# Issuing the second weight part earlier, and one unit's turn, scores and outputs later, in a fused attention and FFN kernel

## The chip, the cores and the metric

One core of one Trainium2 chip. The metric is the device time of one execution in microseconds (us); lower is better. The kernel before takes 318.6 us (median of the first four runs, 318.35 to 320.92).

## The reference, cut to what matters

```python
# q, k, v: (8 batches, 8 heads, 576 tokens, 64) float32; w_in (512, 2048), w_out (2048, 512) float32
scores = (q @ k.T) / 8
ret = scores * Dmat          # causal decay: gamma_h ** (i - j) for i >= j, else 0
x = (ret @ v) -> (4608, 512) # heads side by side
h = x @ w_in
g = where(h > 0, h, exp(min(h, 0)) - 1)
out = g @ w_out              # (4608, 512) float32
```

## The kernel before

The kernel cuts the 4608 tokens into 36 *units* of 128. A unit's raw q, k and v (256 KB each) are loaded by SP's DMA queue. ACT, DVE or POOL cast q and k to bf16, and POOL scales v. PE *turns* q and k (eight transposes, copied out of PSUM by DVE and ACT), makes the *scores*, and the *outputs* (three sets of matmuls named inter, state and intra), which DVE multiplies into `x`. FFN1 follows for a group of units: per tile four matmuls with one 128-column slice of w_in each, then `e` on ACT, `m` on POOL and `g` on DVE. FFN2 follows that. Weights are cast while they are loaded, on POOL's DMA queue, w_in in four parts of 512 columns. The first group is units 0 to 2, and its FFN1 has 16 tiles of 384 tokens, called tile 0 to tile 15 here. Tiles 0 to 3 need w_in part 1, tiles 4 to 7 part 2, and so on. (In the code the parts are numbered from 0.)

The order in which the program lists an engine's instructions is what the change moves. The parts that matter:

```python
def load(u, after=None):                    # SP queue: q, k, v of unit u
    qk = raw.tile(...); vv = raw.tile(...)
    if after is not None:
        after.memset(qk[0:1, 0, 0, 0:1], 0.0)   # holds the load back until this engine is here
    ...
    nc.sync.dma_start(dst, src[...])        # 256 B runs
def load_w_in(n):                           # POOL queue, float32 -> bf16
    nc.gpsimd.dma_start(w_in_sb[:, :, s], w_in_v[:, :, s])
...
for u in range(4):
    load(u)
...                                         # constants
def finish(n=0):                            # g of the tiles that are n slots old, on DVE; frees the tile's bank
    while late and late[0][0] <= slot[0] - n:
        ...
        nc.vector.scalar_tensor_tensor(gt_, ph, 0.0, m, ALU.max, ALU.min)
...
def dummy(n):                               # matmuls that only keep PE busy
    dum = ps_m.tile([P, 512], FP32, name="dum", tag="pm")
...
for u in range(3):
    scores(u); inter(u); state(u); masks(u)
    if u < 2:
        cast(u + 1, A, G)
        if u == 0:
            load_w_in(0)
        scale_v(u + 1)
        dummy(3)
        turn(u + 1, h)
    else:
        for n in range(1, 4):
            load_w_in(n)
        load_w_out(0, 0, 8); load_w_out(0, 8, 16); load_w_out(1, 0, 16)
        dummy(3)
    intra(u); put_x(u); state_out(u); dummy(2)
cast(3, A, V)                               # unit 3: q on ACT, k on DVE, ahead of every e and g below
for n in range(16):                         # tiles 0 to 15
    f1(0, n, m if n % 4 == 3 else None)     # three "h" banks, and "m" for every fourth tile
    if n == 3: turn(3)
    if n == 5: scale_v(3)
    if n == 7: scores(3); masks(3, 0)
    if n == 8: masks(3, 1)
    if n == 9: load(4, nc.vector) ...       # units 4 to 11
    if n == 11: product(3)
for n in range(4):
    f1(1, n, m if n == 3 else None)         # FFN1 of unit 3
finish()
for u, bank in enumerate((h, h, h, m)): ffn2_half(u, 0, bank)
prep(4, A, G); ffn2_half(0, 1, h); turn(4); ...
```

`cast(3, A, V)` stands ahead of the FFN1 tiles in the program. ACT and DVE therefore do nothing for these tiles before unit 3's q and k have landed. A tile's PSUM bank comes free only when DVE has made its `g`, and there are four banks, so tile 4 cannot start before DVE is past its cast.

Of the kernel before, what the change touches and what calls it, by code (L numbers as in the profile page):

```python
# [9 lines left out]
FP32 = mybir.dt.float32  # L10
# [7 lines left out]
def kernel(  # L18
# [14 lines left out]
    P = 128  # L33
# [3 lines left out]
    NU = B * S // P  # L37
# [8 lines left out]
    PE_TURNED = 12  # L46
# [23 lines left out]
    ps_m = ctx.enter_context(tc.tile_pool(name="ps_m", bufs=1, space=PSUM))  # L70
    ps_s = ctx.enter_context(tc.tile_pool(name="ps_s", bufs=1, space=PSUM))
# [22 lines left out]
    def load_w_in(n):  # L94
        s = slice(n * 512, (n + 1) * 512)
        nc.gpsimd.dma_start(w_in_sb[:, :, s], w_in_v[:, :, s])
# [65 lines left out]
    def cast(u, *engs):  # L162

        rqk, _ = raws[u]
        n = nat.tile([P, 2, H * D], BF16, name="qkn", tag="qkn")
        src = rqk.rearrange("p c h d -> p c (h d)")
        if len(engs) == 1:
            engs[0](n, src)  # L168
        else:
            for c in range(2):  # L170
                engs[c](n[:, c], src[:, c])
        kns[u] = n

    def scale_v(u):
        _, rv = raws[u]
        n = nat.tile([P, H, D], BF16, name="vn", tag="vn")
        nc.gpsimd.tensor_tensor(  # L177
            n, rv, gk[:, u % R].unsqueeze(2).to_broadcast([P, H, D]), ALU.mult
        )
        vns[u] = n  # L180

    def turn(u, bank=None):

        t = tpool.tile([P, 2, HP, P], BF16, name="qkT", tag="qkT")
        n = kns[u]
        if u < PE_TURNED:
            if bank:
                pool, tag = bank
                ps = [pool.tile([P, HP, P], BF16, name="tr", tag=tag) for c in range(2)]
            else:  # L190
                both = ps_s.tile([P, 2, 2, HP, P], BF16, name="tr", tag="sc")
                ps = [both[:, c, 0] for c in range(2)]
            for c in range(2):
                for hp in range(HP):
                    nc.tensor.transpose(ps[c][:, hp], n[:, c, hp * P : (hp + 1) * P], ident)  # L195
            nc.vector.tensor_copy(t[:, 0], ps[0])  # L196
            nc.scalar.copy(t[:, 1], ps[1])  # L197
        else:
            nc.sync.dma_start_transpose(
                t.rearrange("p c h t -> p (c h) t"), n.rearrange("p c f -> p (c f)")  # L200
            )
        qkTs[u] = t

    def scores(u):
        t = qkTs[u]
        sc = ps_s.tile([P, 2, HP, P], FP32, name="sc", tag="sc")
        for hp in range(HP):
            for j in range(2):
                for i in range(2):
                    r = slice(i * D, (i + 1) * D)  # L210
                    nc.tensor.matmul(  # L211
                        sc[j * 64 : (j + 1) * 64, i, hp], t[r, 1, hp, j * 64 : (j + 1) * 64], t[r, 0, hp],
                        start=(hp == 0), stop=(hp == HP - 1), skip_group_check=True,
                    )
        scs[u] = sc

    def masks(u, i=None):

        if u not in pts:
            pts[u] = ppool.tile([P, 2, HP, P], BF16, name="pt", tag="pt")  # L220
        m = mask[:, 1 if u % R == 4 else 0]
        s = slice(0, 2) if i is None else slice(i, i + 1)
        nc.vector.tensor_tensor(  # L223
            pts[u][:, s].rearrange("p i h t -> p (i h) t"), scs[u][:, s].rearrange("p i h t -> p (i h) t"),
            m.unsqueeze(1).to_broadcast([P, (s.stop - s.start) * HP, P]), ALU.mult,
        )

    def inter(u):

        o = ps_o.tile([P, HP, P], FP32, name="o", tag="o")  # L230
        os_[u] = o
        r = u % R
        if r == 0:
            return
        n = 64 if r == 4 else P
        for hp in range(HP):
            for i in range(2):
                rows = slice(i * D, (i + 1) * D)
                nc.tensor.matmul(  # L239
                    o[rows, hp, :n], sbs[u][rows, hp], qkTs[u][rows, 0, hp, :n],  # L240
                    start=(hp == 0), stop=False, skip_group_check=True,
                )

    def state(u):

        r = u % R
        if r == 8:
            return
        if r in (0, 4):
            sts[0] = ps_st.tile([P, HP, D], FP32, name="st", tag="st")  # L250
        st = sts[0]
        rows = slice(64, P) if r == 4 else slice(0, P)
        for hp in range(HP):
            for i in range(2):
                h = 2 * hp + i
                nc.tensor.matmul(  # L256
                    st[i * D : (i + 1) * D, hp], kns[u][rows, 1, h * D : (h + 1) * D], vns[u][rows, h],
                    start=(hp == 0 and r in (0, 4)), stop=(r in (3, 7)), skip_group_check=True,
                )

    def state_out(u):
        if u % R == 8:
            return
        s = ppool.tile([P, HP, D], BF16, name="sb", tag="sb")
        nc.scalar.copy(s, sts[0])  # L265
        sbs[u + 1] = s

    def intra(u):
        o = os_[u]
        for hp in range(HP):  # L270
            for i in range(2):
                h = 2 * hp + i
                nc.tensor.matmul(  # L273
                    o[i * D : (i + 1) * D, hp], vns[u][:, h], pts[u][:, i, hp],
                    start=(u % R == 0 and hp == 0), stop=(hp == HP - 1), skip_group_check=True,
                )
# [3 lines left out]
    def put_x(u):  # L280
        g, i = group_of[u]
        if i == 0:
            xts[g] = xpool.tile([P, KJ, 512], BF16, name="xt", tag="xt")
        r = u % R
        s0 = P * r if r < 5 else 64 + P * (r - 5)
        nc.vector.tensor_tensor(  # L286
            xts[g][:, :, i * P : (i + 1) * P], os_[u], gx[:, :, s0 : s0 + P], ALU.mult
        )

    def stretch(u, ahead=True):  # L290

        ahead = ahead and u + 1 < NU
        if ahead:
            scores(u + 1)
        inter(u)
        state(u)
        intra(u)
        if ahead:
            masks(u + 1)
        put_x(u)  # L300
        state_out(u)


# [74 lines left out]
    def ffn2_half(u, c, bank):  # L378
        ffn2_cols(u, c * 256, c * 256 + 256, bank, A if u % 2 else V, nc.scalar)


    V, A, G = nc.vector.tensor_copy, nc.scalar.copy, nc.gpsimd.tensor_copy

    def dummy(n):
        dum = ps_m.tile([P, 512], FP32, name="dum", tag="pm")
        for _ in range(n):
            nc.tensor.matmul(dum, warm[:, :P], warm, start=True, stop=True)  # L387

    def prep(u, *engs):
        if u < NU:  # L390
            cast(u, *engs)
            scale_v(u)
# [8 lines left out]
    def product(u):  # L401
        inter(u)
        state(u)
        intra(u)
        put_x(u)
        state_out(u)

    h, m = (ps_h, "ph"), (ps_m, "pm")


    dummy(18)
    cast(0, A, V)
    make_gx()
    scale_v(0)
    turn(0, h)
    dummy(2)
    for u in range(3):
        scores(u)
        inter(u)
        state(u)  # L420
        masks(u)
        if u < 2:
            cast(u + 1, A, G)
            if u == 0:
                load_w_in(0)
            scale_v(u + 1)
            dummy(3)
            turn(u + 1, h)
        else:
            for n in range(1, 4):  # L430
                load_w_in(n)
            load_w_out(0, 0, 8)
            load_w_out(0, 8, 16)
            load_w_out(1, 0, 16)
            dummy(3)
        intra(u)
        put_x(u)
        state_out(u)
        dummy(2)
# [3 lines left out]
    def f1(g, n, bank=None):  # L443
        k = 512 // (P * len(GROUPS[g]))
        ffn1(g, k * n, bank)

    for n in range(16):
        f1(0, n, m if n % 4 == 3 else None)
        if n == 3:
            turn(3)  # L450
        if n == 5:
            scale_v(3)
        if n == 7:
            scores(3)
            masks(3, 0)
        if n == 8:
            masks(3, 1)
        if n == 9:
            load(4, nc.vector)
            for u in range(5, 12):  # L460
                load(u)
        if n == 11:
            product(3)
    for n in range(4):
        f1(1, n, m if n == 3 else None)
    finish()
# [8 lines left out]
    prep(5, A, G)  # L475
    ffn2_half(2, 1, h)
    product(4)
    turn(5)
    ffn2_half(3, 1, m)
    scores(5)  # L480
    masks(5)
    prep(6, A, G)
    f1(2, 0)
    f1(2, 1)
    turn(6)
    f1(2, 2)


    slots, start, now = [(f1, 2, 3, 1.0)], {}, 1.0
# [38 lines left out]
    for f, g, s, d in slots:  # L528
        while events and events[0][0] <= now + d / 2:
            _, kind, u = events.pop(0)  # L530
# [11 lines left out]
    u = NU - 1  # L542
# [31 lines left out]
```

## Time and profile before

| | before |
|---|---|
| median of runs | 318.6 us |
| span of the profiled execution | 318.0 us |
| PE busy | 307.1 us, 97% |
| chain of waits: PE's share | 82% |
| PE idle before tile 4 (timeline) | 2.26 us |
| unit 3's k cast on DVE | 19.4 us |
| FFN1 of unit 3 done, FFN2 begins | 37.9 us |

These lines are from the page of the kernel before: the busy time of each engine with its share of the span, the busy tenths of PE in 40 slices of the span, the granted PE clock in tenths of full speed in the same slices, and the engines' shares of the chain that ended last.

```profile
PE 307.1 (97%) x2974; PEld 174.2 (55%) x3011; DVE 187.4 (59%) x297; ACT 136.9 (43%) x254; POOL 144.9 (46%) x223
...
PE   8969999999999999999999999999999999999995
...
PEclk9998999999999999999999999999999999999999
...
PE 82%; DMA 6%; issue 3%; POOL 3%; SPq 2%; DVE 2%; ACT 0%; POOLq 0%; DVEq 0%
```

PE is the bound, and it is full except in the first slices. A slice is 8 us. In the third (16 to 24 us) PE was busy six tenths, and in the fourth (24 to 32 us) the clock digit is 8: PE idled first and then ran below full speed.

The next lines are PE's timeline of the kernel before: start, duration, line and operation, and in brackets the idle time just before and what ended it. L329 is an FFN1 matmul, L195 a turn and L370 an FFN2 half.

```profile
17.56 2.76 PE L329 MATMUL ph<-xt,w_in_sb 128*128 128x384 bf16 x16 [0.24 <-DVE xt L286]
20.15 0.61 PE L195 MATMUL tr<-ident,qkn 128*128 128x128 bf16 x8
23.02 4.46 PE L329 MATMUL ph<-xt,w_in_sb 128*128 128x384 bf16 x16 [2.26 <-DMA w_in_sb<-in_moe_w_in_dram]
...
37.92 8.90 PE L370 MATMUL pmh<-w_out_sb,g 128*128 128x256 bf16 x80
```

Tiles 0 to 3 (16 matmuls) end near 20.3 us, the turn of unit 3 fills 0.6 us, and PE then waits for w_in part 2. Tiles 4 to 7 take 4.46 us from 23.02, where tiles 0 to 3 took 2.76 us: most of them ran at half speed.

DVE's timeline of the kernel before shows the cast of unit 3's k with its DMA, and the first two `g`:

```profile
19.40 0.72 DVE L171 CAST qkn<-rqk 128x512 bf16<-128x512 f32 x1 [1.90 <-DMA rqk<-in_k_dram]
20.51 1.04 DVE L313 SCALAR_TENSOR_TENSOR g<-ph,m 128x384 bf16<-128x384 f32 x2 [0.39 <-POOL m L336]
```

Last, the DMA queues of the kernel before in two stretches of one microsecond, 14 to 15 us and 16 to 17 us: packets, MB, and their time as a share of 16 engines. q0 carries the weights, q1 the raw tiles.

```profile
q0 software_dynamic: 156, 0.16, 93.6%
q1 hardware_dynamic: 153, 0.04, 29.6%
```

```profile
q1 hardware_dynamic: 1088, 0.27, 124.2%
```

Beside weight packets of 1 KB, q1 moved 153 packets of 256 B. Alone it moved 1088. Unit 3's 3 x 1,024 packets went through mostly while q0 was empty, from about 15.5 to 17.9 us.

### The profile page before, as it was taken

What the parts mean: (1) busy time and instruction counts of PE and PEld (TensorE: products, weight loads), DVE (VectorE), ACT (ScalarE), POOL (GpSimd) and SP (SyncE); (2) the same over time, 40 slices, a digit from 0 to 9 for tenths busy, and PEclk for the clock granted to TensorE, in tenths of its full rate; (3) what the DMA queues carried; (4) which work ended last, traced back from release to release, by engine and by line L of the source; (5) the groups of instructions that cost most, each with busy time, mean ns of one, the idle gap of its engine ahead of it and who ended that gap; (6) DMA issues with size and microseconds to landing.
All of it is one profiled execution on the core that took longest, in us unless ns stands there. A gap on an engine that the chain in (4) does not pass through costs nothing.

```text
span 318.0 us, 7546 instructions
## 1 busy us (share of the span) xinstructions
PE 307.1 (97%) x2974; PEld 174.2 (55%) x3011; DVE 187.4 (59%) x297; ACT 136.9 (43%) x254; POOL 144.9 (46%) x223
## 2 busy tenths in 40 slices
PE   8969999999999999999999999999999999999995
PEld 3535888877766555555444444444444444444444
DVE  2755724667768777776677666666666655444300
ACT  6435514654643444444444444344444444344411
POOL 2875633555645655544554444444444433333300
PEclk9998999999999999999999999999999999999999
DMA  9999999999999998999999859778224200000111
GB/s 170 215 220 201 197 206 253 205 202 202 207 233 188 233 224 179 168 235 195 170 212 170 171 123 207 166 166 170 69 66 69 66 35 33 35 33 33 66 69 66
DMA packets 150195, 48.72 MB, mean 153 GB/s; under 512 B 138640, under 2 KB 146192, under 8 KB 150160
## 3 DMA queue, kind: packets, MB, share of 16 engines
q1 hardware_dynamic: 141888, 41.76, 67.5%
q0 software_dynamic: 6256, 4.19, 8.8%
q10 hardware_dynamic: 2016, 2.29, 2.2%
q8 instruction: 23, 0.38, 0.5%
q14 instruction: 12, 0.10, 0.1%
HBM read 36.70 MB, written 9.44 MB: 145 GB/s over the span
## 4 chain that ended last, share of the span: by engine, by line
PE 82%; DMA 6%; issue 3%; POOL 3%; SPq 2%; DVE 2%; ACT 0%; POOLq 0%; DVEq 0%
PE ph L329 35%; PE pm L354 31%; PE pmh L370 6%; PE sc L211 3%; DMA w_in_sb<-in_moe_w_in_dram 3%; PE o L273 2%; SPq L86 2%; PE st L256 2%; PE o L239 2%; DMA rv<-in_v_dram 2%; DMA qkT<-qkn 1%; POOL m L336 1%; POOL vn L177 1%; DVE pt L223 1%; PE tr L195 1%
## 5 line engine op out<-in xcount | busy, mean ns | idle before, releaser
L336 POOL TENSOR_SCALAR m<-e 128x512 bf16<-128x512 f32 (+1 forms) x156 | 93.7, 601 | 142.0 <-ACT e L334 137.1
L329 PE MATMUL ph<-xt,w_in_sb 128*128 128x512 bf16 (+3 forms) x816 | 146.5, 315 | 3.9 <-DMA w_in_sb<-in_moe_w_in_dram 2.3
L313 DVE SCALAR_TENSOR_TENSOR g<-ph,m 128x512 bf16<-128x512 f32 (+1 forms) x156 | 100.2, 647 | 81.3 <-POOL m L336 80.3
L334 ACT ACTIVATE e<-ph 128x512 f32<-128x512 f32 (+1 forms) x156 | 87.9, 564 | 124.6 <-PE ph L329 119.8
L354 PE MATMUL pm<-w_out_sb,g 128*128 128x512 bf16 x478 | 122.8, 379 | 1.5 <-issue 0.8
L329 PEld LDWEIGHTS <-w_in_sb 128*128 128x128 bf16 x832 | 71.8, 98 | 59.5 <-issue 4.0
L354 PEld LDWEIGHTS <-g 128*128 128x128 bf16 x496 | 47.8, 98 | 53.2 <-issue 0.2
L223 DVE TENSOR_TENSOR pt<-sc,mask 128x1024 bf16<-128x1024 f32 (+1 forms) x37 | 44.2, 1194 | 14.6 <-PE sc L211 14.4
L177 POOL TENSOR_TENSOR vn<-rv,gk 128x512 bf16<-128x512 f32 x36 | 37.9, 1052 | 1.8 <-DMA rv<-in_v_dram 1.3
L286 DVE TENSOR_TENSOR xt<-o,gx 128x512 bf16<-128x512 f32 x36 | 24.5, 682 | 3.1 <-PE o L273 2.9
L361 ACT COPY ot<-pm 128x512 f32<-128x512 f32 x31 | 18.1, 585 | 14.5 <-PE pm L354 13.8
L370 PE MATMUL pmh<-w_out_sb,g 128*128 128x256 bf16 (+1 forms) x176 | 18.3, 263 | 0.0
L265 ACT CAST sb<-st 128x256 bf16<-128x256 f32 x32 | 11.9, 373 | 13.1 <-PE st L256 11.3
L211 PEld LDWEIGHTS <-qkT 64*64 64x64 bf16 x576 | 9.2, 106 | 14.0 <-issue 7.8
L370 PEld LDWEIGHTS <-g 128*128 128x128 bf16 x176 | 15.7, 98 | 1.9
L168 DVE CAST qkn<-rqk 128x1024 bf16<-128x1024 f32 x24 | 16.6, 691 | 0.0
L211 PE MATMUL sc<-qkT 64*64 64x128 bf16 x576 | 15.1, 222 | 0.7 <-ACT qkT L197 0.5
L273 PE MATMUL o<-pt,vn 128*64 128x128 bf16 x288 | 14.4, 222 | 0.0
L375 DVE COPY oth<-pmh 128x256 f32<-128x256 f32 (+1 forms) x6 | 2.4, 400 | 18.0 <-PE pmh L370 18.0
L387 PE MATMUL dum<-warm 128*128 128x512 bf16 x32 | 11.2, 473 | 1.4 <-DVE warm L108 1.3
L239 PE MATMUL o<-qkT,sb 64*64 64x128 bf16 (+1 forms) x256 | 12.3, 214 | 0.0
L197 ACT COPY qkT<-tr 128x512 bf16<-128x512 bf16 x12 | 7.0, 585 | 9.6 <-DVE qkT L196 5.9
(40 smaller groups left out, 90.1 us busy)
## 6 DMA issues: line engine op xcount, KB each, us to landing
rqk<-in_q_dram SPq DMA_DIRECT2D x32, 256.0 KB, 4.7
rqk<-in_k_dram SPq DMA_DIRECT2D x32, 256.0 KB, 5.0
rv<-in_v_dram SPq DMA_DIRECT2D x32, 256.0 KB, 5.1
out_dram<-ot SPq DMA_DIRECT2D x27, 256.0 KB, 2.3
w_in_sb<-in_moe_w_in_dram POOLq DMA_DIRECT2D x4, 512.0 KB, 9.2
out_dram<-oth ACTq DMA_DIRECT2D x9, 128.0 KB, 4.0
w_out_sb<-in_moe_w_out_dram POOLq DMA_DIRECT2D x2, 512.0 KB, 14.6
w_out_sb<-in_moe_w_out_dram POOLq DMA_DIRECT2D x1, 1024.0 KB, 22.9
```

What stands on the lines that cost most here:

```text
L177: nc.gpsimd.tensor_tensor(n, rv, gk[:, u % R].unsqueeze(2).to_broadcast([P, H, D]), ALU.mult)
L211: nc.tensor.matmul(sc[j * 64 : (j + 1) * 64, i, hp], t[r, 1, hp, j * 64 : (j + 1) * 64], t[r, 0, hp], start=(hp == 0), stop=(hp == HP - 1) ...
L223: nc.vector.tensor_tensor(pts[u][:, s].rearrange("p i h t -> p (i h) t"), scs[u][:, s].rearrange("p i h t -> p (i h) t"), m.unsqueeze(1).t ...
L239: nc.tensor.matmul(o[rows, hp, :n], sbs[u][rows, hp], qkTs[u][rows, 0, hp, :n], start=(hp == 0), stop=False, skip_group_check=True,)
L273: nc.tensor.matmul(o[i * D : (i + 1) * D, hp], vns[u][:, h], pts[u][:, i, hp], start=(u % R == 0 and hp == 0), stop=(hp == HP - 1), skip_g ...
L286: nc.vector.tensor_tensor(xts[g][:, :, i * P : (i + 1) * P], os_[u], gx[:, :, s0 : s0 + P], ALU.mult)
L313: nc.vector.scalar_tensor_tensor(gt_, ph, 0.0, m, ALU.max, ALU.min)
L329: nc.tensor.matmul(ph[:, i * n : (i + 1) * n], w_in_sb[:, j, f : f + P], xts[g][:, j, :n], start=(j == 0), stop=(j == KJ - 1), skip_group_ ...
L334: nc.scalar.activation(e[:, w], ph[:, w], AF.Exp)
L336: nc.gpsimd.tensor_scalar(m[:, w], e[:, w], -1.0, 1.0, ALU.add, ALU.mult)
L354: nc.tensor.matmul(pm, gts[g, ft][:, it * P : (it + 1) * P], w_out_sb[:, ft], start=(ft == 0), stop=(ft == NFT - 1))
L370: nc.tensor.matmul(pm, gts[g, ft][:, it * P : (it + 1) * P], w_out_sb[:, ft, c0:c1], start=(ft == 0), stop=(ft == NFT - 1),)
```

## The change

The intent is to end PE's wait before tile 4. The second w_in part is issued right behind the first. Unit 3's turn, scores and outputs move some tiles later, because its raw tiles will be later. Two pairs of dummies go into the waits that are left. In the later units the order of scores, masks and `x` changes too.

```diff
+def dummy(n, bank=(ps_m, "pm")):            # was: always the "pm" bank
 for u in range(3):
     scores(u); inter(u)
-    state(u)
     masks(u)
     if u < 2:
         cast(u + 1, A, G)
         if u == 0:
             load_w_in(0)
+            load_w_in(1)
         ...
     else:
-        for n in range(1, 4):
+        for n in range(2, 4):
             load_w_in(n)
         ...
+    state(u)
     intra(u) ...
 for n in range(16):
     f1(0, n, ...)
-    if n == 3: turn(3)
+    if n == 3: dummy(2, (ps_s, "sc"))
     if n == 5: scale_v(3)
-    if n == 7: scores(3); masks(3, 0)
-    if n == 8: masks(3, 1)
+    if n == 7: turn(3); dummy(2, (ps_s, "sc"))
     ...
-    if n == 11: product(3)
+    if n == 11: scores(3); masks(3, 0)
+    if n == 12: masks(3, 1)
+product(3)
 ... cut: in stretch(), for units turned on PE, scores(u + 1) and masks(u + 1) go behind intra(u) and put_x(u);
 ... FFN2 halves, turns and scores of units 5 and 6 change places
```

More of the change, by code (lines that the diff above doesn't have):

```diff
@@ L288, in put_x, with stretch @@
         )
-    def stretch(u, ahead=True):
-        ahead = ahead and u + 1 < NU
-        if ahead:
+    def stretch(u):
+        turned = u + 1 < PE_TURNED
+        if u + 1 < NU and not turned:
             scores(u + 1)
@@ L297, in stretch @@
         intra(u)
-        if ahead:
+        if turned:
+            scores(u + 1)
+            put_x(u)
             masks(u + 1)
-        put_x(u)
+        else:
+            if u + 1 < NU:
+                masks(u + 1)
+            put_x(u)
         state_out(u)
@@ L382 @@
     V, A, G = nc.vector.tensor_copy, nc.scalar.copy, nc.gpsimd.tensor_copy
-    def dummy(n):
-        dum = ps_m.tile([P, 512], FP32, name="dum", tag="pm")
+    def dummy(n, bank=(ps_m, "pm")):
+        dum = bank[0].tile([P, 512], FP32, name="dum", tag=bank[1])
         for _ in range(n):
@@ L449 @@
         if n == 3:
-            turn(3)
+            dummy(2, (ps_s, "sc"))
         if n == 5:
@@ L453 @@
         if n == 7:
-            scores(3)
-            masks(3, 0)
-        if n == 8:
-            masks(3, 1)
+            turn(3)
+            dummy(2, (ps_s, "sc"))
         if n == 9:
@@ L462 @@
         if n == 11:
-            product(3)
+            scores(3)
+            masks(3, 0)
+        if n == 12:
+            masks(3, 1)
+    product(3)
     for n in range(4):
@@ L477 @@
     product(4)
+    ffn2_half(3, 1, m)
+    f1(2, 0)
     turn(5)
-    ffn2_half(3, 1, m)
+    prep(6, A, G)
+    f1(2, 1)
     scores(5)
     masks(5)
-    prep(6, A, G)
-    f1(2, 0)
-    f1(2, 1)
+    f1(2, 2)
     turn(6)
-    f1(2, 2)
     slots, start, now = [(f1, 2, 3, 1.0)], {}, 1.0
```

## The prediction

> What bounds the kernel. PE is busy 97% of 318 us (engine table) and is 82% of the chain of waits, so only what idles or slows PE counts. The one large hole is at the start: the timeline has PE idle 2.26 us before 23.02, released by the second w_in part (issued 14.62, landed 22.98). The next eleven or so FFN1 matmuls take 0.32 us instead of 0.16 (granted clock 0.83 in the window 20 to 30), about 1.8 us more. The hole costs about 4 us. The Trainium skill, "TensorE: Matmul & The Clock Gate", part 1, says that idling halves the clock until some 3.4 us of work; here the half-speed stretch is 3.6 us.
>
> Intent: w_in part 2, issued near 10.7, lands near 20, before tile 4 wants it (20.7). Four dummies cost 0.2 us each, partly inside waits.
>
> What I think it does. The DMA rings are full (share over 1.0 from 2 us on). By quarter microseconds the DMA view shows, from 14.0 to 15.25, 40 packets of the weight queue to 40 of the raw-load queue: round robin by packet, as the skill's "DMA: Bandwidth & Descriptors", queues section, has it. But weight packets are 1 KB and raw-load packets 256 B, so raw loads get 160 packets/us beside weights, against 1,080 alone. Before, unit 3's raw tiles (3 x 1,024 packets) pass through a gap in the weight queue from 15.5 to 17.9: q landed 18.2, k 19.4. Now the second part fills that gap: 1,024 weight packets from 12.2 last until about 18.7, and the third part (still issued 14.6, 3.3 us to its first packet) is waiting by 18. So unit 3's q should land near 21, its k near 26 to 28 (240 packets/us beside w_out's 512 B packets from 25), its v near 31.
>
> The change did not move unit 3's casts: ACT's comes before the first exponential, DVE's (the k half) before the first g. DVE would sit before that cast until about 27, so no h bank is freed, and tile 4 (which needs tile 0's bank) starts near 28 instead of 23.0, on a cold clock: about +5 us. Then the dummies behind the turn share the turn's bank and wait for its two copies (about 1 us), and the product right before f1(1,0) exposes its 0.69 us multiply. f1(1,0) started near 34.3 before; I expect 39 to 42.5.
>
> Gains: putting x before the masks in turned units frees x 1.2 us earlier (the mask multiply's time); the PE waits it can remove between 50 and 100 us total about 0.5 us. From 100 us on nothing changes; PE is bound and absorbs nothing.
>
> Sum: about +8 us if the gap closes fully, +3 to +5 if a gap in the weight queue remains, -2 if unit 3's loads are hardly delayed. I weight these 0.5, 0.25, 0.25. Predicted 324.5 us, 317 to 328. Faster by over 2%: 0.03; within 2%: 0.50; slower by over 2%: 0.47.
>
> Right would show as: waits list a long "DVE qkn <- DMA rqk k" (5 us or more), PE's tile 4 released by DVE g, not by w_in; weight queue without gap from 12 to 34; low clock from 28 to 32; PE waiting before the dummies after the turn and before f1(1,0). Wrong: unit 3's k cast before 22 us, PE idle under 1 us at tile 4.
>
> What would make it wrong: the third part's descriptors starting later than 18.7, so raw loads slip through; arbitration that favours raw loads when two weight parts queue.

## The result, and the profile after

The changed kernel takes 330.56 us (median of four runs, 329.87 to 330.92) against 318.6 us. The ratio is 1.0358, with a 95% interval of 1.0314 to 1.0401: slower. A ratio here is the mean time of one kernel's runs over that of the other's runs of the same rounds, so it is not quite the ratio of the medians. Executions over 1.5% slower than the fastest of the same kernel are left out of the means.

These are the page's lines of the changed kernel, the same four as before:

```profile
PE 308.7 (94%) x2978; PEld 174.9 (53%) x3015; DVE 186.8 (57%) x297; ACT 136.7 (42%) x254; POOL 144.7 (44%) x223
...
PE   8944889999999999999999999999999999999996
...
PEclk9995999999999999999999999999999999999999
...
PE 86%; DMA 5%; SPq 3%; DVE 3%; issue 1%; ACT 1%; DVEq 0%
```

PE's work is the same (308.7 against 307.1 us busy), but the third and fourth PE digits fell to 4, and the fourth clock digit is 5.

PE's timeline of the changed kernel follows; its line numbers are five higher (L334 is FFN1, L392 a dummy, L375 an FFN2 half).

```profile
17.52 2.76 PE L334 MATMUL ph<-xt,w_in_sb 128*128 128x384 bf16 x16 [0.24 <-DVE xt L286]
20.33 0.38 PE L392 MATMUL dum<-warm 128*128 128x512 bf16 x1
29.26 4.71 PE L334 MATMUL ph<-xt,w_in_sb 128*128 128x384 bf16 x16 [8.55 <-DVE g L318]
...
35.55 0.59 PE L392 MATMUL dum<-warm 128*128 128x512 bf16 x2 [1.13 <-ACT qkT L197]
...
43.82 3.73 PE L334 MATMUL ph<-xt,w_in_sb 128*128 128x128 bf16 x64 [0.79 <-DVE xt L286]
47.39 8.90 PE L375 MATMUL pmh<-w_out_sb,g 128*128 128x256 bf16 x80
```

Tile 4 now starts at 29.26 us instead of 23.02, and DVE's `g` is what it waited for, not w_in. Tiles 4 to 7 again run partly at half speed: the trace's clock record has the granted clock at 0.5 from 23.0 to 33.3 us. Behind the turn, PE waits 1.13 us before the dummies. The first matmul of unit 3's FFN1 waits 0.79 us for `x`. The FFN2 halves begin at 47.39 us instead of 37.92. Of the 10.2 us by which the two profiled spans differ, 9.47 us are there by this point.

DVE's timeline of the changed kernel, the same two groups:

```profile
28.31 0.43 DVE L171 CAST qkn<-rqk 128x512 bf16<-128x512 f32 x1 [10.85 <-DMA rqk<-in_k_dram]
28.65 1.95 DVE L318 SCALAR_TENSOR_TENSOR g<-ph,m 128x384 bf16<-128x384 f32 x4
```

DVE stood still for 10.85 us in front of unit 3's k, and 28.31 replaces 19.40. The DMA queues of the changed kernel from 16 to 17 us show why the k was late:

```profile
q0 software_dynamic: 147, 0.15, 88.7%
q1 hardware_dynamic: 144, 0.04, 28.5%
```

Weight packets now fill the microsecond that belonged to the raw tiles before, and q1 moves 144 packets instead of 1088. Finally, PE's waits in the changed kernel, by total, number and longest:

```profile
PE ph L334 <- DVE g L318: 8.8, 2, 8.5
...
PE dum L392 <- ACT qkT L197: 1.1, 1, 1.1
PE ph L334 <- DVE xt L286: 1.0, 2, 0.8
```

The first line is the loss at tile 4, the second the wait in front of the dummies, the third that for unit 3's `x`.

### The profile page after: what moved, and what is told of

It is laid out like the page before. It is cut to its first block, busy times and chain, and to the rows that moved or that the text cites. A ratio compares the mean times of both kernels' runs of the same rounds, so it can differ in the third digit from the quotient of the medians.

```text
span 328.2 us, 7558 instructions
## 1 busy us (share of the span) xinstructions
PE 308.7 (94%) x2978; PEld 174.9 (53%) x3015; DVE 186.8 (57%) x297; ACT 136.7 (42%) x254; POOL 144.7 (44%) x223
## 4 chain that ended last, share of the span: by engine, by line
PE 86%; DMA 5%; SPq 3%; DVE 3%; issue 1%; ACT 1%; DVEq 0%
PE ph L334 37%; PE pm L359 32%; PE pmh L375 5%; DMA rqk<-in_k_dram 5%; PE sc L211 4%; SPq L86 3%; PE o L273 2%; PE o L239 2%; PE st L256 2%; PE tr L195 1%; DVE pt L223 1%; DVE g L318 1%; ACT qkT L197 1%; DVE qkT L196 0%; DVE xt L286 0%
## 5 line engine op out<-in xcount | busy, mean ns | idle before, releaser
L334 PE MATMUL ph<-xt,w_in_sb 128*128 128x512 bf16 (+3 forms) x816 | 146.9, 315 | 10.8 <-DVE g L318 8.8
L334 PEld LDWEIGHTS <-w_in_sb 128*128 128x128 bf16 x832 | 72.2, 98 | 66.6 <-issue 13.3
L375 PE MATMUL pmh<-w_out_sb,g 128*128 128x256 bf16 (+1 forms) x176 | 18.3, 263 | 0.0
L265 ACT CAST sb<-st 128x256 bf16<-128x256 f32 x32 | 11.9, 373 | 13.1 <-PE st L256 11.3
L375 PEld LDWEIGHTS <-g 128*128 128x128 bf16 x176 | 15.7, 98 | 2.0
L392 PE MATMUL dum<-warm 128*128 128x512 bf16 x36 | 11.8, 457 | 2.5 <-DVE warm L108 1.3
```

The lines of the kernel that those rows point to most:

```text
L334: nc.tensor.matmul(ph[:, i * n : (i + 1) * n], w_in_sb[:, j, f : f + P], xts[g][:, j, :n], start=(j == 0), stop=(j == KJ - 1), skip_group_ ...
L375: nc.tensor.matmul(pm, gts[g, ft][:, it * P : (it + 1) * P], w_out_sb[:, ft, c0:c1], start=(ft == 0), stop=(ft == NFT - 1),)
```

## The experiments

The theory: the early second part takes the time in which unit 3's raw tiles passed, and because engines work in order, DVE holds up `g`, banks and tile 4 behind unit 3's cast. The first rival: the later turn, scores and outputs, with the dummies, cost the time. A second rival: the weights or the raw tiles are late for another reason. Each ratio is against the kernel before, measured in the same rounds.

| run | what | median us | ratio (95%) |
|---|---|---|---|
| e1_w1_back | the change without the early second part | 323.24 | 1.0131 (1.0093 to 1.0169) |
| e2_w1_only | before, with the early second part alone | 326.27 | 1.0213 (1.0167 to 1.0259) |
| e3_cast_late | the change, unit 3's casts just before its turn | 327.06 | 1.0241 (1.0203 to 1.0279) |
| e4_turn_late | the change, unit 3's casts and turn after tile 11 | 325.34 | 1.0188 (1.0135 to 1.0241) |
| e5_w2_early | the change, third part early too | 330.12 | 1.0320 (1.0288 to 1.0351) |
| e6_k3_on_act | the change, unit 3's k on ACT's queue | 328.01 | 1.0250 (1.0219 to 1.0281) |
| e7_late_only | before, with the later units' order alone | 320.86 | 1.0036 (0.9996 to 1.0077) |
| e8_warm | before, with dummies in the old hole | 321.26 (all six runs, one of them slow) | 1.0011 (0.9970 to 1.0052) |
| e9_warm_v_late | e8, v scaling later | 319.42 | 1.0012 (0.9993 to 1.0031) |
| e10_moves_only | before, with unit 3's moves and dummies alone | 322.98 | 1.0126 (1.0108 to 1.0144) |
| e11_w1_back_v_late | e1, v scaling later | 323.80 | 1.0168 (1.0141 to 1.0196) |
| e12_pause | the change, a pause in the weight queue forced | 333.68 | 1.0468 (1.0450 to 1.0486) |
| e13_warm_cast4 | e9, unit 4's q cast on DVE | 318.62 | 0.9990 (0.9972 to 1.0008) |
| e14_cast4_only | before, unit 4's q cast on DVE | 318.31 | 0.9993 (0.9968 to 1.0018) |
| e15_warm_cast45 | e13, unit 5's q cast on DVE too | 318.17 | 0.9983 (0.9966 to 1.0001) |

All gave correct results. By a rule of 2%, e3, e5, e6 and e12 are slower than the kernel before, e2 and e4 are unclear, because their intervals contain 2%, and the others count as the same. The intervals of e1, e2, e4, e10 and e11 lie wholly above 1, so these are slower too, by an amount that may be under 2%.

### e1_w1_back and e2_w1_only: the two halves of the change

```diff
 # e1, from the changed kernel
             load_w_in(0)
-            load_w_in(1)
-        for n in range(2, 4):
+        for n in range(1, 4):
 # e2, from the kernel before
             load_w_in(0)
+            load_w_in(1)
-        for n in range(1, 4):
+        for n in range(2, 4):
```

> The changed kernel, with only the second w_in part put back to its old place (issued with the third and fourth, after unit 2's v scaling). Theory (the early second part takes the gap through which unit 3's raw tiles landed): unit 3's k cast on DVE comes back from 28.3 us to about 19.4 us, PE's tile 4 is again released by the w_in DMA near 23.0 us, and the run falls from 330.6 to about 320 to 322 us (what is left over the kernel before: turn 0.45, wait for its copies 1.1, dummies 0.4, multiply before f1(1,0) 0.8, late section 0.5). Rival (the later turn, scores, outputs and the dummies cost the time): the run stays above 327 us.

> The kernel before, with only the second w_in part issued right behind the first. Theory: unit 3's k cast near 28.3 us, PE's tile 4 near 29.4 us instead of 23.0, run 325 to 327 us (+6.5 to +8). Rival (the rest of the change costs the time): the w_in wait goes and the run is 314 to 319 us.

Measured: e2, with the early second part alone, loses 7.5 us (326.27 against 318.79 us). Taking that part out of the change (e1) brings 330.56 down to 323.24 us. PE's timeline of e2:

```profile
23.83 0.60 PE L195 MATMUL tr<-ident,qkn 128*128 128x128 bf16 x4 [2.95 <-ACT qkn L171]
29.34 0.61 PE L195 MATMUL tr<-ident,qkn 128*128 128x128 bf16 x4 [4.91 <-DVE qkn L171]
29.80 2.72 PE L329 MATMUL ph<-xt,w_in_sb 128*128 128x384 bf16 x8
```

The four transposes of k wait for DVE's cast until 29.34 us and tile 4 follows at 29.80, as the theory had it. DVE's timeline of e1:

```profile
19.14 1.13 DVE L171 CAST qkn<-rqk 128x512 bf16<-128x512 f32 x1 [1.51 <-DMA rqk<-in_k_dram]
```

In e1 DVE's cast is back at 19.14 us and tile 4 at 21.89. But e1 is 4.4 us above the kernel before, where I expected 1 to 3 us. The two halves add up (7.5 and 4.4 to the measured 11.9), so the first rival is partly right: the moves cost as well, and more than I had put down.

### e3_cast_late: the cast's place in the order

```diff
-cast(3, A, V)                       # ahead of the tiles
     if n == 7:
+        cast(3, A, V)
         turn(3); dummy(2, (ps_s, "sc"))
-    if n == 5: scale_v(3)
+    if n == 11: ...; scale_v(3)
```

> The changed kernel with unit 3's casts moved from ahead of the FFN1 tiles to just before its turn (after tile 7), and its v scaling after tile 11; the DMA order is untouched. Theory (the loss comes through DVE and ACT, which take their work in order, standing before unit 3's casts): k still lands near 28.3 us, but tile 4 starts near 20.8 us without waiting for DVE; the wait moves to the turn after tile 7, tile 8 starts near 31.3 us instead of 36.0, run 326 to 328 us. Rival (tile 4 would have waited for w_in or for a bank anyway): tile 4 stays near 29 us and the run near 330 us.

PE's timeline of e3, with tiles 4 to 7 and the k half of the turn:

```profile
20.62 2.76 PE L334 MATMUL ph<-xt,w_in_sb 128*128 128x384 bf16 x16
...
28.78 0.61 PE L195 MATMUL tr<-ident,qkn 128*128 128x128 bf16 x4 [3.85 <-DVE qkn L171]
```

With the same loads in the same order, tile 4 starts at 20.62 us with no wait. The k still comes at 28.3 us (DVE's cast starts at 28.30), and now the turn waits for it. Tile 8 starts at 31.33 us, and the run is 327.06 us, as expected. So DVE's order turned the late k into a late tile 4. The late k itself costs time wherever it is first wanted.

### e4_turn_late: wanting unit 3 later still

```diff
-    if n == 7: turn(3); dummy(2, (ps_s, "sc"))
-    if n == 11: scores(3); masks(3, 0)
-    if n == 12: masks(3, 1)
+    if n == 11: cast(3, A, V); turn(3)
+    if n == 13: scores(3); masks(3, 0)
+    if n == 14: masks(3, 1)
+scale_v(3)
 product(3)                          # and no cast(3) or scale_v(3) further up
```

> The changed kernel with unit 3's casts and turn after tile 11, its scores after tile 13, its v scaling after tile 15. Theory: with nothing of unit 3 wanted before its k has landed (28.3 us), tiles 4 to 11 run as w_in lands, no wait over 3.5 us is left on PE, f1(1,0) starts near 35.5 us instead of 43.8 and the run is 319 to 322 us. Rival (the weights themselves come later in the changed order): tile 8 or 12 waits for w_in beyond 29 us and the run stays above 325 us.

The start is as expected: the FFN1 of unit 3 begins at 35.88 us (expected 35.5). The time is not: 325.34 us against 319 to 322. PE then waits 2.77 us for ACT's cast of unit 4's q, and the FFN2 half behind that takes 3.21 us instead of 1.92, with the granted clock at 0.5 from 51.2 to 54.6 us. Time won back at the start was partly lost 15 us later. That was a first hint that the start is not paced by PE alone.

### e5_w2_early, e6_k3_on_act and e12_pause: what makes the k late

```diff
 # e5, from the changed kernel
             load_w_in(1)
+            load_w_in(2)
-        for n in range(2, 4):
+        for n in range(3, 4):
 # e6, from the changed kernel: load(3) no longer issues k on SP; in the loop over units 0 to 2
         turn(u + 1, h)
+        if u == 1: load(3, part="k")        # nc.scalar.dma_start
 # e12, from the changed kernel
+            nc.gpsimd.tensor_copy(gate, raws[3][0][:, 1, 0, 0:1])   # waits for unit 3's k
             for n in range(2, 4): load_w_in(n)
-            load_w_out(0, 0, 8); load_w_out(0, 8, 16); load_w_out(1, 0, 16)
     if n == 7:
+        load_w_out(0, 0, 8); load_w_out(0, 8, 16); load_w_out(1, 0, 16)
         turn(3); ...
```

> The changed kernel with the third w_in part issued early too, right behind the second. In the changed kernel the weight queue pauses near 18.8 to 19.4 us and unit 3's tiles move about 700 packets in that microsecond. Theory (unit 3's tiles move at 160 packets/us beside 1 KB weight packets and quickly only in a pause): the pause goes, unit 3's k is cast near 30 us instead of 28.3, tile 4 starts 1.5 to 2.5 us later and the run is 332 to 333 us. Rival (unit 3's load is slow for a reason of its own, such as its issue, not for want of a pause): k stays at 28.3 us and the run at 330.6 us.

e5 missed, and the numbers that its rival named came true. In the changed kernel q1 moves 701 packets between 18.5 and 19.5 us, in a short pause of the weight queue. In e5 this pause is gone (158 packets from 19 to 20 us). Yet the k is cast at 28.29 us, the same as in the changed kernel, and the time is the same. Counted from 13 us, q1's first 2,048 packets, about the q and k of unit 3, had started by about 24 us in the changed kernel and by about 27 us in e5, and yet both k landed near 28.3. The packets that passed in the short pause did not help.

The Trainium skill, "DMA: Bandwidth & Descriptors", section "Why a DMA increments its semaphore by 16 and not by 1", says that a DMA runs on up to 16 engines that finish independently and has landed only when all have. The packed traces keep the time of each of the 16 increments, which the views do not print, and they agree. In the changed kernel those for unit 3's k begin at 21.71 us; the fifteenth comes at 26.44 and the last at 28.29. In e5 the first fifteen come between 27.05 and 27.48 us and the last at 28.27. So the pause made fifteen parts of the load earlier and left the last one where it was, and the landing is that of the last. Part 2 of w_in has such a straggler as well (fifteenth increment at 19.55 us, last at 20.40). If both are one DMA engine, it was still at weights during the pause. The increments do not name the engines, so this stays argued. The rival's reason, a load that is slow through its own issue, is ruled out by e12 below.

> The changed kernel with one load moved to another queue: unit 3's k is issued by ACT (after unit 2's turn, near 14.5 us) instead of by SP behind unit 3's q. Nothing else moves. Theory (packets are shared out round robin by queue, so what counts for k is its queue and its place in it): k has a share of its own, lands near 23 to 25 us instead of 28.3, the DVE cast and tile 4 move up by 4 to 5 us, and the run is 325 to 327.5 us. Rival (the rings share bytes, or the slow engines decide, whichever queue is used): k lands at 27 us or later and the run stays above 329 us.

The DMA queues of e6 from 21 to 22 us, with q10 as ACT's queue:

```profile
q0 software_dynamic: 134, 0.14, 80.4%
q1 hardware_dynamic: 135, 0.03, 25.9%
q10 hardware_dynamic: 133, 0.03, 15.3%
```

The three queues move nearly the same number of packets. The k, with a share of its own, is cast at 26.13 us instead of 28.31, and the run is 328.0 us, between the two expectations. My time was off because the k's first packets moved near 18 us, 4 us after ACT issued it, and not 1 to 2 us after.

> The changed kernel with a pause in the weight queue put back by force: POOL copies one column of unit 3's k, which makes it wait for k's landing, and only then issues w_in parts 3 and 4; the w_out parts are issued by POOL after tile 7. The second w_in part stays right behind the first. Theory (unit 3's tiles need a time without weight packets on every one of the 16 rings): k lands by 22.5 us instead of 28.3, tile 4 starts at 24 to 25.5 us instead of 29.3, and the run is 324 to 327.5 us in spite of the later weights. Rival (unit 3's tiles are late for another reason, such as their issue or the second part alone): k at 26 us or later.

DVE's and PE's timelines of e12:

```profile
21.89 0.43 DVE L171 CAST qkn<-rqk 128x512 bf16<-128x512 f32 x1 [4.03 <-DMA rqk<-in_k_dram]
```

```profile
25.05 4.09 PE L334 MATMUL ph<-xt,w_in_sb 128*128 128x384 bf16 x16 [3.94 <-DVE g L318]
...
58.05 1.03 PE L195 MATMUL tr<-ident,qkn 128*128 128x128 bf16 x8 [5.17 <-ACT qkn L171]
```

With a full pause (1,039 raw packets from 19 to 20 us) and the second part still right behind the first, the k is cast at 21.89 us and tile 4 starts at 25.05. Both are as the theory expected, so want of a pause is what made the k late. The run is nevertheless slower than the changed kernel. The w_out parts, issued from 31 us on, now share the queues with unit 4's raw tiles and the first outputs, and the turn of unit 4 waits 5.17 us. That the first brings the second is my reading of the trace; no run separates it. My expected time for the whole run was wrong by 6 us or more.

### e7_late_only and e10_moves_only: the rest of the change

```diff
 # e7: before, plus only these parts of the change
+stretch(): scores(u + 1), masks(u + 1) behind intra(u), put_x(u);  FFN2 halves and units 5, 6 in the new order
 # e10: before, plus only these
+state(u) later;  dummies after tiles 3 and 7;  turn(3) after tile 7;  scores(3) after 11;  product(3) after 15
```

> The kernel before with only the last part of the change: x before the masks and scores after the outputs in the units turned on PE, and the new order of FFN2 halves, turns and scores of units 5 and 6. Prediction on record: gain of about 0.5 us. Reading of the changed kernel's trace: three PE waits of 0.24, 0.33 and 0.32 us between 65 and 70 us against one of 0.24 us before, so a loss of 0.4 to 0.8 us (319.0 to 319.6 us). Rival: no difference.

> The kernel before with only unit 3's turn, scores and outputs and the state products moved and the dummies added, as in the change; loads, the order inside the later units and the order of units 4 to 6 as before. Theory (what e1_w1_back lost, 4.4 us, comes from these moves: turn 0.45 us out of the old wait, 1.1 us until its copies free the dummies' bank, dummies 0.4, 0.8 us for the multiply before f1(1,0), POOL before unit 3's v 1.6): 322 to 323.5 us. Rival (the later units' order is the larger part): below 320.5 us.

e7 is the same within 2%, and its interval (0.9996 to 1.0077) allows both no loss and a small one. A gain of the predicted 0.5 us lies outside it. Its six executions fall in two groups: 319.27 to 319.85 us at a clock of 1.0, and 321.87 to 322.85 us at 0.995. The first group is no slower than the kernel before (median 319.96 us in these rounds). e10 is clear: the moves cost 4.1 us (322.98 against 318.85). PE's timeline of e10:

```profile
25.28 0.61 PE L195 MATMUL tr<-ident,qkn 128*128 128x128 bf16 x8
27.02 0.59 PE L387 MATMUL dum<-warm 128*128 128x512 bf16 x2 [1.13 <-ACT qkT L197]
...
35.29 3.73 PE L329 MATMUL ph<-xt,w_in_sb 128*128 128x128 bf16 x64 [0.79 <-DVE xt L286]
...
49.20 0.62 PE L195 MATMUL tr<-ident,qkn 128*128 128x128 bf16 x8 [1.44 <-ACT qkn L171]
```

The sum is 0.45 us for the turn (the start-to-start time of its eight transposes), which before stood in the wait for w_in and was free; 1.13 us until its copies free the dummies' bank; 0.43 us of dummies; 0.79 us for `x`; and 1.44 us before the turn of unit 4. That makes 4.2 us, near the 4.1 of the medians. It is a list from one trace and counts a little too much: that execution lost 3.2 us (322.05 against 318.85). In e7's profile, whose program is that of before up to the turn of unit 4, this turn starts at 45.91 us after a wait of 0.60 us already, and in e10 it starts 3.3 us later.

### e8_warm, e9_warm_v_late and e11_w1_back_v_late: what the old hole was worth

```diff
 # e8, from the kernel before
     if n == 3:
+        dummy(7, (ps_s, "sc"))
         turn(3)
 # e9, from e8
-    if n == 5: scale_v(3)
+    if n == 8: ...; scale_v(3)
 # e11, from e1
-    if n == 5: scale_v(3)
+    if n == 11: ...; scale_v(3)
```

> The kernel before with seven dummy matmuls (1.5 us) after tile 3, ahead of unit 3's turn, in PE's wait for the second w_in part; no load moves. Theory (of the hole's 4 us some 1.8 us are the halved clock after 2.3 us of idling, not the wait itself): tiles 4 to 7 take 2.8 us instead of 4.5, and the run is 316.5 to 317.5 us. Rival (the clock does not matter, since w_in parts 3 and 4 pace the tiles behind): 318.5 us or more.

In e8 tiles 4 to 7 run at full clock (2.76 us), and the run gained nothing. My theory fell here. But e8 did not get rid of the half clock: in its profile the clock falls to 0.5 at 30.12 us, behind the next wait, for 3.41 us, and four of the six executions have a clock of 0.995. e9 is the cleaner test, with a clock of 1.0 in all six. PE's and POOL's timelines of e8:

```profile
22.41 2.76 PE L329 MATMUL ph<-xt,w_in_sb 128*128 128x384 bf16 x16
...
29.24 0.81 PE L329 MATMUL ph<-xt,w_in_sb 128*128 128x384 bf16 x4 [2.32 <-DVE g L313]
```

```profile
27.08 1.04 POOL L177 TENSOR_TENSOR vn<-rv,gk 128x512 bf16<-128x512 f32 x1 [1.97 <-DMA rv<-in_v_dram]
```

PE waits 2.32 us before tile 10, because POOL stands before the scaling of unit 3's v, which lands at 27.1 us.

> The kernel before with the seven dummies of the run named e8_warm and unit 3's v scaling three FFN1 tiles later (after tile 8 instead of 5). In e8_warm POOL stood 1.97 us before that scaling until v had landed (27.1 us), and PE's tile 10 then waited 2.32 us for a g. Theory (the start is paced by a row of landings, so taking one wait away shows the next): PE's wait at tile 10 goes, f1(1,0) starts near 32 us, but the turn of unit 4 then waits for its casts (unit 4's raw tiles land near 45.5 us whatever PE does), and the run gains 0 to 1% (316.5 to 319 us). Rival (PE's idle time at the start counts in full): the run gains the 2.5 us or more by which f1(1,0) is earlier, all the way to the end.

e9 moves that scaling. The FFN2 halves begin at 35.70 us instead of 37.92, and the next wait appears. PE's timeline of e9:

```profile
46.11 0.62 PE L195 MATMUL tr<-ident,qkn 128*128 128x128 bf16 x8 [1.09 <-ACT qkn L171]
```

The time is that of the kernel before (1.0012). So e9 took 2.2 us off the start of the profiled execution of before and gave all of it back. Against e7's profile, in which the clock stayed at 1.0, FFN2 began only 0.7 us earlier (35.70 against 36.41): most of the 2.2 us is the half clock, which few executions of before have.

> The run e1_w1_back with unit 3's v scaling moved from after tile 5 to after tile 11. Theory: POOL's 3.0 us wait for unit 3's v, and with it PE's 1.6 us wait for a g before tile 10, go; f1(1,0) starts near 34.7 us instead of 36.3; run 321.5 to 322.5 us against 323.2. Rival: no change, since a later landing paces it (unit 4's raw tiles).

e11 tells the same. The wait at tile 10 goes, but the wait for unit 4's cast grows from 0.70 to 2.49 us, and the run is no faster (323.80 against 323.24 us). The rival was right.

### e13_warm_cast4, e14_cast4_only and e15_warm_cast45: the next wait

```diff
 # e13, from e9; e14, from the kernel before
-prep(4, A, G)
+prep(4, V, G)
 # e15, from e13
-prep(5, A, G)
+prep(5, V, G)
```

> The run e9_warm_v_late with unit 4's q cast on DVE instead of ACT. In e9 PE's turn of unit 4 waited 1.09 us (to 46.1 us) for ACT's cast, and ACT stood 4.79 us before it in the copies and issues of the FFN2 outputs, whose DMA issue alone took 3.04 us. Theory (e9's gain at the start was lost to this wait): the turn of unit 4 starts near 44.5 to 45 us and the run falls below the kernel before by 0.3 to 0.8%. Rival (unit 4's raw tiles themselves land too late): the turn stays near 46 us and the run within 0.2% of before.

> The kernel before with only unit 4's q cast on DVE. Theory (in the kernel before the start is late enough that the turn of unit 4 seldom waits): within 0.3% of before, so that the start and this wait have to be mended together. Rival (this wait alone bounds the first 50 us): as fast as e13_warm_cast4.

> As e13_warm_cast4, and unit 5's q cast on DVE too (ACT waited 0.78 us for unit 5's q in e9, which delays its copies of the FFN2 outputs). Theory: 0 to 0.3% below e13. Rival: the cast holds up DVE's score mask and is slower.

PE's timeline of e13:

```profile
44.71 0.61 PE L195 MATMUL tr<-ident,qkn 128*128 128x128 bf16 x8
```

With unit 4's q cast on DVE its turn starts at 44.71 us without a wait, so the wait was ACT's chain of output copies and issues, and not the landing of unit 4's tiles alone. That chain is itself paced by landings. The 3.04 us that my expectation put down to two output issues in e9 were mostly waiting, for the issues themselves took 0.34 and 0.40 us. Between them ACT stood at a semaphore (a counter that tells of a DMA's landing) which SP's load of half of unit 4's k used as well, until that load landed at 43.73 us. The next issue, just before the cast, stood until 44.92 us for unit 5's q in the same way.

The gain is smaller than expected: e13 is within 0.3% of before, and e15, the fastest version tried, gains 0.17%, with an interval that just reaches 1. e14 alone does nothing measurable. No version beats the kernel before clearly. In e15's profile (span 316.1 us) PE has no wait over 0.3 us between 20 and 110 us. The profile of before that I read (318.0 us, clock 0.993) was not a typical execution either. In the rounds of all these runs, 5 of 40 executions of before had a clock below 0.998. These five took 0.7 to 2.2 us longer than the mean of the others in their rounds.

## Why the prediction was wrong

The direction and the main mechanism were right, and the size was wrong: 324.5 us with 317 to 328, against 330.56. Point by point:

- "So unit 3's q should land near 21, its k near 26 to 28": near. The q landed at 22.4 us and the k at 28.29. The k's number held partly by luck: it was worked out for a weight queue without a gap. There was a short one, and only the last of the k's 16 increments took no profit from it. e3 and e12 show that this wait and the missing pause were the cause.
- "tile 4 ... starts near 28 instead of 23.0, on a cold clock: about +5 us": right in kind and a little small. It was 29.26, so +6.2 us. With the early part alone, e2 measured +7.5 us for the whole run.
- The step that failed is the sum: "about +8 us if the gap closes fully". The gap closed but for one short pause, and the run lost 12.0 us. Two terms were too small. "About +5 us" for tile 4 measured 7.5 us (e2, with no other part of the change). For the moves the sum held about 1 us for the dummies' wait and 0.7 us for the exposed multiply, less 0.5 us of gains. They cost 4.1 us (e10), and with the later units' order 4.4 us (e1). I had costed the turn at nothing, although it left a wait where it was free. I had costed the dummies as "partly inside waits". The wait of unit 4's turn, which a later start with a changed rhythm brings, I had not seen at all. 7.5 and 4.4 us make 11.9.
- "I weight these 0.5, 0.25, 0.25": the weights pulled the point down to 324.5, which none of the three cases gives. The case "-2 if unit 3's loads are hardly delayed" rested on the next term.
- "The hole costs about 4 us": wrong. In e9 the hole was filled and the clock stayed full, for a gain of nothing. Behind the hole stood unit 3's v (e8), and behind that ACT's chain before unit 4's turn (e9). The half clock does cost time where it occurs, 0.7 to 2.2 us, but 35 of 40 executions of before had a clock of 0.998 or more. The hole itself was also smaller in other profiles with the old order of loads (1.77 us in e7, 1.00 in e14). For most executions the change's aim was therefore a wait worth next to nothing. And 1.5 of the 2.26 us were spent on one straggling part: fifteen of the 16 increments of w_in part 2 had come by 21.46 us and the last came at 22.98.
- "the PE waits it can remove between 50 and 100 us total about 0.5 us": not gained (e7: 1.0036, interval from 0.9996). In the profiles, 0.7 us of the 10.2 us were added after the FFN2 halves began.
- "the third part ... is waiting by 18": near. Its packets were at full rate from 19.5 us, with a short pause before. e5 shows that this pause was of no use to the k. The prediction had named a later third part as what would make it wrong, "so raw loads slip through". 701 packets did slip through in the pause, without moving the k's landing.

Open: whether it is always the same DMA engine that is last, and why. In the kernel before, the last increment begins to lag after 16 us (by 1.2 us for unit 3's k), and at 15.51 us a packet of 16 KB on queue q8, of the kind "instruction", had taken 0.93 us. That the two belong together is a guess. Open too is how much the later units' order costs.

## What to carry to other kernels

Before you issue a load earlier, ask which load passes in the time it will take: a queue of small packets beside one of large packets got its share of packets here, not of bytes (144 of 256 B beside 147 of 1 KB). Before you count an idle gap as gain, look at the next landing and the next engine's chain behind it. Here two further waits stood behind the gap, each ready to take over. And when work moves later "because its data are later", move every engine's share of it: the casts stayed where they were, and the engine that held them held everything behind them.

## What the Trainium skill lacked or had wrong

- "DMA: Bandwidth & Descriptors", section "Queues, rings and completion order", states round robin between queues at packet granularity. The runs agree: 147 to 144 packets in a microsecond with two queues, 134, 135 and 133 with three. It lacks the consequence in bytes: 256 B packets beside 1 KB packets fell from 1088 to 144 packets per microsecond.
- The same page's section "Latency and other measured facts" gives a first byte after about 0.6 us (HWDGE) or 1 us (SWDGE). Under load it was far later here: 3.3 us for w_in part 2 of the kernel before (issued 14.62, first packets near 17.9) and about 4 us for ACT's load in e6 (issued 13.71, packets near 17.9). In e12, with the queues nearly drained, w_in part 3 took 1.5 us (issued 22.30, first packet 23.81).
- No page used here says that a DMA issue can hold its engine for long: SP's issue of unit 3's v took 2.94 us in the kernel before and 6.38 us in the changed one, where the first issue of a run took 0.45 us. Nor does one say that an issue can wait for another engine's load that used the same semaphore: in e9 ACT stood at an output issue until SP's load had landed at 43.73 us.
- "TensorE: Matmul & The Clock Gate", part 1, has the clock drop after an idle window of about 3.4 us, in a free-running window. Here less idling was enough: the clock dropped after 2.26 us in one execution of before and after 1.73 us in e14, and did not after 2.04 us in e11 and 1.88 us in e10. No fixed length of idling divides these; a free-running window would fit. In the clock record the stretch at half speed was 3.41 us in before, as the page has it, and 10.24 us in the changed kernel, where PE idled for the first 6.2 us of it.
